# Any two PSUM banks in one relu or clamp, the low-order product planned by itself, first weights multiplied on four quadrants, and a due time for each tile pair

## The chip, the cores and the metric

The kernel runs on one core of a Trainium2 chip. Its time is what the device takes for one execution, in microseconds (us). The number that counts is the median of several runs. An execution under the hardware profiler gives the trace from which the views below are drawn. The core has five engines with an instruction queue each, all of them in order: TensorE (PE, matrix products; its weight loads are shown as PEld), VectorE (DVE), ScalarE (ACT), GpSimd (POOL) and SyncE (SP, which here only issues DMAs). PE writes its results to PSUM, eight banks of 512 floats in each of 128 partitions; DVE and ACT read PSUM, and POOL works on SBUF alone.

## The reference

The input is 4 batches of 12480 tokens with 128 channels, and 32 inducing vectors. Two attention steps are followed by a two-layer network:

```python
def mab(q, kv):
    s = scale * (q @ kv.transpose(0, 2, 1))
    s = s - s.max(-1, keepdims=True)
    a = np.exp(s)
    a /= a.sum(-1, keepdims=True) + 1e-09
    return a @ kv
h = mab(I, x)              # 32 summaries of each batch
y = mab(x, h)              # each token attends to the summaries
z = y.reshape(49920, 128) @ w_in            # 128 -> 2048
g = np.where(z >= 1, z, np.where(z <= -1, 0.0, (z + 1) ** 2 / 4))
out = g @ w_out                             # 2048 -> 128
```

## The kernel before, in words

**Chunks and pairs.** The tokens are cut into 104 chunks of 480 (26 in each batch). The summaries `hT` of a batch are multiplied with `w_in` first, so that the first layer needs only the 32 attention weights of each token: its right side is `hw`, 32 rows for `w_in`'s 2048 columns, kept as an upper and a lower part. The 128 rows of an `hw` tile are two copies of the upper part and two of the lower, and the 128 rows of a chunk's `aT` are upper, lower, upper, lower part of the attention weights, so that one product of 128 rows sums all four. `aT` is filled by four DMAs of 32 rows each, from `a` and `ahi`.

For each chunk there are eight pairs of column tiles, 832 pairs in all. A pair is made in these steps:

1. PE writes two hidden tiles of 128x480 into two PSUM banks (L774).
2. ACT adds 1 and takes the relu of each bank into one half of an SBUF tile `w` (L782).
3. ACT squares all of `w` with a factor of one half (L768).
4. DVE clamps: w = min(max(bank, 1), w) (L787). The two banks are free after that.
5. For six of the eight pairs (`SPLIT`), `w` is rounded to the format fp32r as `hi`, by DVE (L810), ACT (L807) or POOL (L805), and POOL makes `lo` = w - hi (L813).
6. PE adds the pair to the chunk's accumulator (L844): for each half three products, w_lo x hi, w_hi x hi and w_hi x lo; for the two other pairs one product in full float precision, which the trace shows as two records.

There is one accumulator bank. After the last product of a chunk DVE transposes it into `oT` (L854), SP stores it with four DMAs (L858), and only then may the next chunk's first product start. The other seven banks ("h") hold hidden tiles and the scores and summaries of the attention.

**One wide instruction for two banks.** Step 2 and step 4 can be done for both halves in one instruction of 960 elements. Before, that happens only if the two banks are an even one and the next (0 and 1, 2 and 3, 4 and 5), and if both halves are ready when the first is picked; `Slot.pick` looks for such neighbours. Otherwise two instructions of 480 are written.

**The order of the work** is made by a planner when the program is built (`Plan.order`). Each piece of work is added with its engine, an assumed cost, a due time, the work it needs, and the buffer slots it uses. The planner walks through an assumed time; whenever an engine is free it takes, of the work that can start, the one with the smallest due time. Pieces with several engines to choose from (`hi`, and the copy `eN`) go to the engine that gets to them first by this rule. Its result is a fixed list of instructions for each engine; on the chip each engine works through its list and waits for semaphores. Due times before are `STEP` times the pair's number plus an offset from `BEHIND`, one for each kind of work.

**The summaries.** While a batch's chunks run, the next batch is loaded and summarized (`summarize`), and its `hw` tiles are made: four products of 128x512 with `hT` repeated four times over the 128 columns (L634), each cast by ACT (L640), and the lower half of each corrected by DVE (L644). `attend` makes the attention weights of four chunks at a time.

Of the kernel before, what the change touches and what calls it, by code (L numbers as in the profile page):

```python
# [20 lines left out]
    h=7, o=1, xn=9, xT=26, xr=2, e1=1, eN=1, hw=6, w=8, hi=4, lo=4, aT=3, s2=2, a=1, ahi=1, oT=1  # L21
# [8 lines left out]
LEAD = 66950  # L30
STEPS = [0, 1200, 2400, 3600, 8000, 12000, 13000, 18000, 24000, 28000, 32000]

SC = [0, 1200, 2400]
GA = [0, 1500, 6000, 7500]


# [3 lines left out]

KEEP = 0


class Slot:


    def __init__(self, pool, turn=None, near=None):
        self.pool, self.left, self.until, self.place, self.tile = pool, 0, 0, None, None
        self.turn, self.near, self.first = turn, near, False
        if near:  # L50
            near.first = True

    def pick(self, spare, now):

        free = {i for t, i in spare if t <= now}
        if self.near and self.near.place is not None and self.near.place ^ 1 in free:
            return self.near.place ^ 1
        if self.first:
            return min(free, key=lambda i: (i ^ 1 not in free, i % 2, i))
        return min(free, key=lambda i: (i ^ 1 in free, i))  # L60


class Op:


    def __init__(self, engine, cost, lag, due, emit, needs, uses, tiled):
        choice = engine if isinstance(engine, dict) else {engine: (cost, lag, due)}
        self.choice, self.emit, self.uses = choice, emit, uses
        self.engine, self.cost, self.due = None, 0, due
        self.tiled, self.twin, self.merged, self.wide = tiled, None, None, False  # L70
        self.start = self.after = 0
        self.by = {}
        self.unmet, self.then = 0, []
        for n in needs:
            n.then.append(self)
            self.unmet += 1
        for s in self.uses:
            s.left += 1

    def ready(self, engine):  # L80
        return max([self.after, *(t for e, t in self.by.items() if e == engine)])

    def beside(self):

        a, b = self.uses[0].place, self.twin.uses[0].place
        return a % 2 == 0 and b == a + 1


class Plan:
# [5 lines left out]
    def add(self, engine, cost, lag, due, emit, needs=(), uses=(), tiled=False):  # L95
        op = Op(engine, cost, lag, due, emit, [n for n in needs if n], uses, tiled)
        self.ops.append(op)
        return op

    @staticmethod  # L100
    def twins(a, b, cost, lag):

        a.twin, b.twin, a.merged = b, a, (cost, lag)

    def order(self):
        engines = sorted({e for op in self.ops for e in op.choice})
        free = dict.fromkeys(engines, 0)
        able = {e: [] for e in engines}

# [3 lines left out]

        for op in self.ops:
            if not op.unmet:
                enable(op)
        spare = {p: [(0, i) for i in range(n)] for p, n in SLOTS.items()}
        turn = dict.fromkeys(SLOTS, 0)
        tiled = False
        now, done = 0, []  # L120
        while len(done) < len(self.ops):
            later = []
            took = False
            for e in engines:
# [3 lines left out]
                best, rank = None, 0  # L128
                for op in able[e]:
# [12 lines left out]
                    due = op.choice[e][2] - (KEEP if e == "PE" and op.tiled == tiled else 0)  # L142
                    if best is None or due < rank:
                        best, rank = op, due
# [6 lines left out]
                for s in best.uses:  # L151
                    if s.place is None:
                        s.place = s.pick(spare[s.pool], now)
# [3 lines left out]
                if best.merged and best.beside():  # L157
# [6 lines left out]
                if e == "PE" and best.tiled != tiled:  # L164
                    cost, lag, tiled = cost + RETILE, lag + RETILE, best.tiled
                for op in both:
                    op.start, op.engine, op.cost, op.lag = now, e, 0, lag
                    done.append(op)
                best.cost = cost
                free[e] = now + cost  # L170
                later.append(free[e])
                for s in [s for op in both for s in op.uses]:
                    s.left -= 1
                    s.until = max(s.until, now + lag)
                    if not s.left:
                        spare[s.pool].append((s.until, s.place))
                for n in [n for op in both for n in op.then]:
                    n.unmet -= 1
                    if list(n.choice) == [e]:
                        n.after = max(n.after, now + cost + RAW[e])  # L180
                    elif e in n.choice:
                        for x in n.choice:
                            n.by[x] = max(n.by.get(x, 0), now + cost + RAW[e] if x == e else now + lag)
                    else:
                        n.after = max(n.after, now + lag)
                    if not n.unmet:
                        enable(n)
# [7 lines left out]
def attn_moe(  # L195
# [38 lines left out]
        xr=([C, NB, M], F32), e1=([P, CW], F32), eN=([96, 5, P], F32), hw=([P, 512], F32R),  # L234
# [23 lines left out]

    turns = dict.fromkeys(SLOTS, 0)

    def in_turn(pool, near=None):
        turns[pool] += 1
        return Slot(pool, turns[pool] - 1, near)
# [651 lines left out]
```

## Time and profile before

| What | Value |
|---|---|
| median of 3 runs (lowest to highest) | 1773.66 us (1773.36 to 1774.67) |
| the profiled execution | 1771.55 us, of which the trace spans 1769.7 us |
| busy: PE, PEld | 1717.7 us (97%), 1226.7 us (69%) |
| busy: ACT, DVE, POOL | 1695.4 us (96%), 1622.8 us (92%), 1610.4 us (91%) |
| ACT busy in the first 80 us | 9.15 + 12.96 + 4.98 + 11.77 us |
| first relu of a hidden tile on ACT | 72.87 us after the start |
| start of the last square on ACT | 1754.71 us after the start |

PE's matmul records overlap, because one starts before the one ahead of it has left the pipeline, so its busy share is no measure of how full it is; ACT's and DVE's records overlap a little in the same way. How long an engine is held by an instruction is better read as the pitch: the time from its start to the start of the next one, where no wait lies between. The first 75 us load and summarize the first batch. From about 100 us on all engines run the pairs.

### The profile page before, as it was taken

The numbers are of one execution on the slowest core, as the hardware profiler recorded it, in microseconds if no ns is written. First come the engines' busy times: TensorE is split into PE (matmuls) and PEld (weight loads), VectorE is DVE, ScalarE is ACT, GpSimd is POOL, SyncE is SP. The second block draws the span as 40 slices with busy tenths as digits, with TensorE's granted clock in tenths as the row PEclk, the third lists the DMA queues.
The fourth block names the chain that finished last, engine by engine and source line by source line (L and its number), as shares of the span: only waits on it lengthen the run. The fifth ranks groups of instructions, "written<-read, shape, count | busy, mean of one in ns | idle before, by whom it ended". The sixth has DMA issues, their size and how long they took to land.

```text
span 1769.7 us, 26019 instructions
## 1 busy us (share of the span) xinstructions
PE 1717.7 (97%) x7898; PEld 1226.7 (69%) x7898; DVE 1622.8 (92%) x2393; ACT 1695.4 (96%) x2658; POOL 1610.4 (91%) x863
## 2 busy tenths in 40 slices
PE   7699999999999999999999999999999999999998
PEld 5467677777767677776767777677776777777676
DVE  7899889998899898999889999899889999999996
ACT  5599999999999999999999999999999999999997
POOL 0499999999899999999999999999998999999997
PEclk9699999999999999999999999999999999999999
DMA  9532423423232343332233423332211111111111
GB/s 243 98 63 56 79 49 60 72 58 60 44 67 49 62 79 59 65 76 48 47 56 61 72 49 64 70 65 51 45 20 38 34 27 30 35 34 34 33 29 17
DMA packets 425069, 101.78 MB, mean 58 GB/s; under 512 B 369602, under 2 KB 420386, under 8 KB 424930
## 3 DMA queue, kind: packets, MB, share of 16 engines
q1 hardware_dynamic: 424834, 100.01, 30.1%
q8 instruction: 62, 1.02, 0.2%
q14 instruction: 77, 0.63, 0.1%
q10 hardware_dynamic: 96, 0.12, 0.0%
HBM read 48.94 MB, written 25.56 MB: 42 GB/s over the span
## 4 chain that ended last, share of the span: by engine, by line
PE 49%; ACT 25%; DVE 13%; issue 7%; POOL 3%; DMA 2%; SPq 1%; DVEq 0%; POOLq 0%; ACTq 0%
PE banks L844 34%; ACT w L782 13%; PE banks L774 10%; ACT w L768 10%; DVE w L787 7%; DVE hi L810 3%; POOL lo L813 2%; ACT hi L807 1%; PE banks L669 1%; DVE oT L854 1%; PE banks L477 1%; PE banks L530 1%; PE banks L634 1%; SPq L455 1%; POOL hi L805 1%
## 5 line engine op out<-in xcount | busy, mean ns | idle before, releaser
L813 POOL TENSOR_TENSOR lo<-w,hi 128x960 fp32r<-128x960 f32 x624 | 1399.7, 2269 | 63.4 <-DVE hi L810 28.4
L787 DVE SCALAR_TENSOR_TENSOR w<-banks,w 128x480 f32<-128x480 f32 (+1 forms) x1428 | 978.0, 729 | 95.5 <-ACT w L768 85.3
L782 ACT ACTIVATE w<-banks 128x480 f32<-128x480 f32 (+1 forms) x1503 | 889.2, 666 | 12.3 <-PE banks L774 9.5
L768 ACT ACTIVATE w<-w 128x960 f32<-128x960 f32 x832 | 867.0, 1066 | 2.2
L774 PE MATMUL banks<-aT,hw 128*128 128x480 f32 x1664 | 594.9, 431 | 18.2 <-DVE w L787 9.9
L844 PE MATMUL banks<-hi,w_lo 128*128 128x480 f32 x1248 | 538.3, 431 | 9.5 <-DVE oT L854 5.7
L844 PE MATMUL banks<-lo,w_hi 128*128 128x480 f32 x1248 | 474.6, 380 | 1.4 <-POOL lo L813 1.4
L844 PE MATMUL banks<-hi,w_hi 128*128 128x480 f32 x1248 | 474.0, 380 | 0.0
L810 DVE TENSOR_REDUCE hi<-w 128x960 fp32r<-128x960 f32 x373 | 423.7, 1140 | 11.7 <-PE banks L844 0.9
L774 PEld LDWEIGHTS banks<-aT,hw 128*128 128x128 f32 x1664 | 306.7, 189 | 184.1 <-DVE w L787 107.1
L844 PE MATMUL banks<-w,w_f 128*128 128x480 f32 x832 | 393.1, 567 | 0.2 <-DVE oT L854 0.2
L844 PEld LDWEIGHTS banks<-hi,w_lo 128*128 128x128 f32 x1248 | 234.9, 188 | 119.9 <-issue 53.4
L844 PEld LDWEIGHTS banks<-hi,w_hi 128*128 128x128 f32 x1248 | 235.3, 189 | 57.6 <-issue 28.9
L844 PEld LDWEIGHTS banks<-lo,w_hi 128*128 128x128 f32 x1248 | 234.5, 188 | 39.6 <-POOL lo L813 2.9
L844 PEld LDWEIGHTS banks<-w,w_f 128*128 128x128 f32 x832 | 156.1, 189 | 62.6 <-issue 44.3
L805 POOL TENSOR_SCALAR hi<-w 128x960 fp32r<-128x960 f32 x145 | 144.4, 999 | 16.3 <-DVE w L787 9.7
L807 ACT CAST hi<-w 128x960 fp32r<-128x960 f32 x106 | 109.6, 1034 | 7.2 <-PE banks L844 3.3
L854 DVE STREAM_TRANSPOSE oT<-banks 128x480 f32<-128x480 f32 x104 | 70.1, 674 | 7.8 <-PE banks L844 7.5
L403 POOL TENSOR_TENSOR w_lo<-hi,w_hi 128x256 fp32r<-128x256 f32 x6 | 6.5, 1076 | 60.6 <-ACT w_hi L405 60.6
L458 DVE STREAM_TRANSPOSE xT<-xr 128x480 f32<-128x480 f32 x78 | 51.2, 663 | 3.1 <-DMA xr<-in_x 3.0
L712 POOL TENSOR_TENSOR a<-a,ahi 128x480 fp32r<-128x480 f32 (+1 forms) x27 | 33.2, 1231 | 1.3 <-ACT ahi L709 1.3
L530 PE MATMUL banks<-xn,eN 120*32 120x128 f32 (+1 forms) x774 | 31.7, 275 | 0.5 <-ACT eN L522 0.5
(82 smaller groups left out, 553.1 us busy)
## 6 DMA issues: line engine op xcount, KB each, us to landing
out<-oT SPq DMA_DIRECT2D x416, 60.0 KB, 2.2
xn<-in_x SPq DMA_DIRECT2D x93, 240.0 KB, 4.2
xr<-in_x SPq DMA_DIRECT2D x312, 60.0 KB, 2.5
aT<-ahi SPq DMA_DIRECT2D x208, 60.0 KB, 2.0
aT<-a SPq DMA_DIRECT2D x206, 60.0 KB, 2.0
w<-in_x SPq DMA_DIRECT2D x11, 240.0 KB, 4.5
w<-in_moe_w_in SPq DMA_DIRECT2D x8, 256.0 KB, 4.5
w<-in_moe_w_out SPq DMA_DIRECT2D x8, 256.0 KB, 5.3
```

Source lines behind the costliest of these rows:

```text
L458: nc.vector.transpose(make(xT[b, c]), xr.tile.rearrange("c n i -> c (n i)"))
L530: nc.tensor.matmul(p[q * M : (q + 1) * M, :C], eN[g].tile[:, t, q * M : (q + 1) * M], xn[g * Q + q].tile[:, t, :], start=(t == 0), stop=(t ...
L768: nc.scalar.activation(w.tile, w.tile, AF.Square, scale=0.5)
L774: nc.tensor.matmul(make(h)[:, :CW], hw[b][ft // 4].tile[:, ft % 4 * P : (ft % 4 + 1) * P], aT[b, c].tile, start=True, stop=True,)
L782: each(of, i, hs_, w, lambda to, h: nc.scalar.activation(to, h, AF.Relu, bias=1.0))
L787: lambda to, h: nc.vector.scalar_tensor_tensor(to, h, 1.0, to, op0=ALU.max, op1=ALU.min),
L805: nc.gpsimd.tensor_scalar(make(hi), w.tile, 1.0, 0.0, op0=ALU.mult, op1=ALU.add)
L807: nc.scalar.copy(make(hi), w.tile)
L810: nc.vector.tensor_reduce(make(hi), w.tile.unsqueeze(3), axis=AX.X, op=ALU.max)
L813: nc.gpsimd.tensor_sub(make(lo), w.tile, hi.tile.bitcast(F32))
L844: nc.tensor.matmul(acc.tile[:, :CW], wt, g, start=(first and n == 0), stop=(last and n == len(terms) - 1),)
L854: nc.vector.transpose(make(oT).rearrange("c n i -> c (n i)"), acc.tile[:, :CW])
```

## The change

**Any two banks.** `Slot.pick` and `Op.beside` are gone. The two banks of a pair may be any two of the seven; a wide instruction reads them with a step from the lower to the higher bank. Which half of `w`, and which of the two column tiles, a bank holds follows from which of the two banks is the lower (`half`). Where a wide instruction isn't possible yet because the second half isn't ready, the first one's due time is put later by `LONE`.

**The low-order product apart.** The products of a split pair are two pieces of work for the planner instead of one: w_lo x hi and w_hi x hi (`p`), which need only `hi`, and w_hi x lo (`pl`), which needs `lo`.

**First weights on quadrants.** `hT` is kept once (32 columns). One piece of work multiplies it with the four 512-column parts of `w_in`, each into its own 32 partitions of one bank; one ACT cast (`hx`) and one DVE subtraction (`hy`) follow; 16 DMAs on SP's queue copy their 32-row parts into the `hw` tiles.

**Due times.** `BEHIND`, `LEAD`, `STEPS`, `SC` and `GA` become one table `DUE`, with a number for each of the eight pairs of a chunk and each kind of work. `KEEP`, which favours PE work of the same tiling as before, goes from 0 to 450, and assumed costs change by a few ns each.

The diff, cut to its core:

```diff
-BEHIND = {
-    "h": -4400, "r": -3050, "s": -700, "t": 400, "hi": 3700, "hi ACT": 14900, "hi POOL": 9600,
-    "lo": 2200, "p": 9300, "ps": 8900,
+DUE = {
+    "h": [-8100, -3450, -2750, -3300, -3950, 1600, -30300, -35450],
+    "r": [5450, 8600, 10700, -1550, 18200, -11550, -13450, -10800],
...
+LONE = {"r": 300, "t": 150}
-    def beside(self):
-
-        a, b = self.uses[0].place, self.twin.uses[0].place
-        return a % 2 == 0 and b == a + 1
...
+                    if op.merged and not (op.twin in able[e] and op.twin.ready(e) <= now):
+                        due += op.lone
...
-                if best.merged and best.beside():
+                if best.merged:
...
     def each(of, i, hs_, w, do):
         if of[i].wide:
-            do(w.tile, banks[:, hs_[0].place : hs_[0].place + 2, :CW])
+            a, b = sorted(h.place for h in hs_)
+            do(w.tile, banks[:, a : b + 1 : b - a, :CW])
         else:
-            do(w.tile[:, i], hs_[i].tile[:, :CW])
+            do(w.tile[:, half(i, hs_)], hs_[i].tile[:, :CW])
...
-                cost, needs, uses = 3 * 217, [l], [hi, lo]
+                parts = [
+                    ([(w_lo, hi), (w_hi, hi)], 436, "p", [u], [hi]),
+                    ([(w_hi, lo)], 218, "pl", [l], [lo]),
+                ]
             else:
-                hi, lo = w, None
-                cost, needs, uses = 804, ts, [w]
+                parts = [([(w_f, w)], 806, "pf", ts, [w])]
...
+        def multiply():
+            p = make(s_w)
+            for k in range(FF // 512):
+                nc.tensor.matmul(
+                    p[k * M : (k + 1) * M], hT[b], w_in_sb[:, k * 512 : (k + 1) * 512], start=True, stop=True
+                )
+        def upper():
+            nc.scalar.copy(make(wide_hi), s_w.tile)
+        def lower():
+            nc.vector.tensor_sub(make(wide_lo), s_w.tile, wide_hi.tile.bitcast(F32))
...
+            def spread(r, k=k, dst=dst):
+                src = (wide_hi if r < 2 else wide_lo).tile[k * M : (k + 1) * M]
+                nc.sync.dma_start((dst.tile or make(dst))[r * M : (r + 1) * M].bitcast(F32), src.bitcast(F32))
```

How the lists of instructions move is shown at three places. The first is ACT's list some way into the first batch (L782 and L814 are the relu, L768 and L800 the square, L807 the rounding). Before:

```order
L768 ACTIVATE w_1410_5192<-w_1410_5192 128x960
L782 ACTIVATE w_1414_5211<-banks_64 128x480
L768 ACTIVATE w_1414_5211<-w_1414_5211 128x960
L782 ACTIVATE w_1423_5242<-banks_64 128x480 x2
L782 ACTIVATE w_1425_5251<-banks_64 128x480
L768 ACTIVATE w_1423_5242<-w_1423_5242 128x960
L782 ACTIVATE w_1425_5251<-banks_64 128x480
L807 CAST hi_1429_5270<-w_1414_5211 128x960
```

And in the changed kernel:

```order
L814 ACTIVATE w_1401_4938<-banks_64 128x480
L800 ACTIVATE w_1398_4930<-w_1398_4930 128x960
L814 ACTIVATE w_1401_4938<-banks_64 128x480
L814 ACTIVATE w_1406_4955<-banks_64 128x480
L800 ACTIVATE w_1401_4938<-w_1401_4938 128x960
L814 ACTIVATE w_1406_4955<-banks_64 128x480
L814 ACTIVATE w_1414_4978<-banks_64 128x960
L800 ACTIVATE w_1406_4955<-w_1406_4955 128x960
L800 ACTIVATE w_1414_4978<-w_1414_4978 128x960
```

Over the whole program ACT's list goes from 1342 relus of 480 and 161 of 960 to 666 and 499, and from 106 roundings to 69; DVE's from 1192 clamps of 480 and 236 of 960 to 832 of 960, and from 373 roundings to 421; POOL's roundings from 145 to 134.

The second place is PE's list where the 40th chunk ends and the 41st begins (L774 and L806 write hidden tiles, L844 and L871 add to the accumulator; `w_hi7` belongs to a chunk's last pair, `w_lo0` to the first of the next). Before:

```order
L844 MATMUL banks_64<-hi_2017_7317,w_hi7_100 128x480
L844 MATMUL banks_64<-lo_2025_7343,w_hi7_100 128x480
L774 MATMUL banks_64<-aT_1908_6923,hw_1353_4985 128x480 x4
L774 MATMUL banks_64<-aT_1952_7103,hw_1320_4883 128x480
L844 MATMUL banks_64<-hi_2019_7330,w_lo0_89 128x480
L844 MATMUL banks_64<-hi_2019_7330,w_hi0_88 128x480
L844 MATMUL banks_64<-lo_2030_7378,w_hi0_88 128x480
```

And in the changed kernel:

```order
L871 MATMUL banks_64<-hi_2018_6987,w_lo7_101 128x480
L871 MATMUL banks_64<-hi_2018_6987,w_hi7_100 128x480
L871 MATMUL banks_64<-lo_2025_7009,w_hi7_100 128x480 x2
L806 MATMUL banks_64<-aT_1907_6616,hw_1331_4699 128x480 x2
L806 MATMUL banks_64<-aT_1907_6616,hw_1342_4737 128x480 x3
L871 MATMUL banks_64<-hi_2023_7003,w_lo0_89 128x480
L871 MATMUL banks_64<-hi_2023_7003,w_hi0_88 128x480
```

Between the last product of a chunk and the first of the next there stand 4.1 matmuls on average over the 103 handovers before (three in 50 of them), and 5.5 in the changed kernel (five in 58 of them). Behind the last `lo` there now come two products instead of the three of each half.

The third place is SP's list ahead of the first chunk: before, the first chunk's `aT` comes right behind the loads of the next batch.

```order
L455 DMA xr_193_939<-in_x 32x15x32 x4
L733 DMA aT_202_973<-ahi_199_966 32x480 x2
L733 DMA aT_203_980<-ahi_199_966 32x480 x2
L733 DMA aT_203_980<-a_198_963 32x480 x2
L733 DMA aT_207_997<-ahi_199_966 32x480 x2
```

In the changed kernel eleven DMAs for `hw` stand ahead of it:

```order
L669 DMA hw_190_934<-hx_188_927 32x512 x2
L669 DMA hw_190_934<-hy_189_932 32x512 x2
L669 DMA hw_193_945<-hx_188_927 32x512 x2
L669 DMA hw_193_945<-hy_189_932 32x512 x2
L669 DMA hw_195_961<-hx_188_927 32x512 x2
L669 DMA hw_195_961<-hy_189_932 32x512
L760 DMA aT_200_978<-ahi_198_968 32x480 x2
```

What moved there is the queue's order: the first hidden tile needs its `hw` tile and its `aT` from the same queue.

More of the change, by code (lines that the diff above doesn't have):

```diff
@@ L165, in order @@
                     cost, lag, tiled = cost + RETILE, lag + RETILE, best.tiled
+                free[e] = now + cost
+                later.append(free[e])
                 for op in both:
@@ L168, in order @@
                     done.append(op)
+                    left -= 1
+                    finish(op, e, cost, lag)
                 best.cost = cost
[L170 to L187, printed above, removed]
             if not took:
```

256 lines of the change are left out of this document (131 added, 125 removed), and 15 rows, old and new, of the table DUE.

## The prediction

> **What bounds the kernel now.** I read the page's busy shares first, then the busy time by stage, then how the engines stand inside the long middle stage. The page says that no engine is free:
>
> ```profile
> PE 1717.7 (97%) x7898; PEld 1226.7 (69%) x7898; DVE 1622.8 (92%) x2393; ACT 1695.4 (96%) x2658; POOL 1610.4 (91%) x863
> ```
>
> The table by stage (columns: length, then busy time of PE, PEld, DVE, ACT, POOL) puts ACT's idle time at the start:
>
> ```profile
> 60.00:80.00 20.00, 12.34 (x36) 5.46 (x34) 16.37 (x30) 11.77 (x22) 5.82 (x7) 0.67 0.27 54
> ...
> 100.00:1700.00 1600.00, 1580.32 (x7047) 1133.02 (x7046) 1488.42 (x2124) 1579.52 (x2451) 1520.41 (x809) 1.00 0.29 53
> ```
>
> From 100 to 1700 us ACT is idle for only 20 us of 1600, POOL for 80, DVE for 112. PE's 1580 says little, since its records overlap. That ACT isn't merely waiting inside its instructions is seen in its timeline (start, length, instruction), where each starts as soon as the one ahead lets it:
>
> ```profile
> 1743.73 0.99 ACT L782 ACTIVATE w<-banks 128x960 f32<-128x960 f32 x1
> 1744.58 1.02 ACT L807 CAST hi<-w 128x960 fp32r<-128x960 f32 x1
> 1745.46 1.07 ACT L782 ACTIVATE w<-banks 128x480 f32<-128x480 f32 x2
> 1746.37 1.05 ACT L768 ACTIVATE w<-w 128x960 f32<-128x960 f32 x1
> 1747.27 1.07 ACT L782 ACTIVATE w<-banks 128x480 f32<-128x480 f32 x2
> ...
> 1754.00 0.68 ACT L782 ACTIVATE w<-banks 128x480 f32<-128x480 f32 x1
> 1754.71 1.00 ACT L768 ACTIVATE w<-w 128x960 f32<-128x960 f32 x1
> ```
>
> The pitches are 0.85 us for a wide relu, 0.88 for a rounding, 0.45 for a single relu (two in 0.91), 0.90 for a square. The last pair of rows shows a price: the square at 1754.71 works on what the relu at 1754.00 has just written, and starts after 0.71 instead of 0.45 us. With the counts in the view of groups,
>
> ```profile
> L813 POOL TENSOR_TENSOR lo<-w,hi 128x960 fp32r<-128x960 f32 x624 | 1399.7, 2269 | 63.4 <-DVE hi L810 28.4 <-ACT hi L807 8.5 <-PE banks L844 7.4
> L768 ACT ACTIVATE w<-w 128x960 f32<-128x960 f32 x832 | 867.0, 1066 | 2.2
> L782 ACT ACTIVATE w<-banks 128x480 f32<-128x480 f32 x1342 | 733.4, 626 | 11.5 <-PE banks L774 8.7 <-DMA aT<-a 1.2
> L782 ACT ACTIVATE w<-banks 128x960 f32<-128x960 f32 x161 | 160.8, 1002 | 0.8 <-PE banks L774 0.8
> L807 ACT CAST hi<-w 128x960 fp32r<-128x960 f32 x106 | 109.6, 1034 | 7.2 <-PE banks L844 3.3 <-DVE w L787 2.7 <-DVE nm L585 0.6
> L805 POOL TENSOR_SCALAR hi<-w 128x960 fp32r<-128x960 f32 x145 | 144.4, 999 | 16.3 <-DVE w L787 9.7 <-PE banks L844 1.3 <-DVE sm L698 1.1
> ```
>
> ACT's pairs hold it for 1342 x 0.45 + 161 x 0.85 + 832 x 0.90 + 106 x 0.88 = 1583 us. For PE I take the pitch of a matmul, 0.22 us, and of a full-precision product, 0.81 us (803.56 to 804.59 is one of those and one hidden tile):
>
> ```profile
> 800.22 0.38 PE L844 MATMUL banks<-hi,w_lo 128*128 128x480 f32 x1
> 800.44 0.38 PE L844 MATMUL banks<-hi,w_hi 128*128 128x480 f32 x1
> ...
> 803.56 0.97 PE L844 MATMUL banks<-w,w_f 128*128 128x480 f32 x2
> 803.99 0.76 PE L774 MATMUL banks<-aT,hw 128*128 128x480 f32 x1
> 804.59 0.38 PE L844 MATMUL banks<-hi,w_lo 128*128 128x480 f32 x1
> ```
>
> A chunk has 16 hidden tiles, 36 split products and 4 full ones: 52 x 0.217 + 4 x 0.81 = 14.5 us (the quoted starts round 0.217), over 104 chunks 1510. PE also has, in its four largest other groups, 99 us:
>
> ```profile
> L477 PE MATMUL banks<-xT,indT 128*32 128x480 f32 x208 | 29.6, 590 | 0.0
> L669 PE MATMUL banks<-xT,hT 128*32 128x480 f32 x208 | 29.1, 595 | 1.4 <-DVE hw L644 1.0 <-DVE hT L614 0.4
> L530 PE MATMUL banks<-xn,eN 120*32 120x128 f32 x624 | 22.7, 276 | 0.0
> L634 PE MATMUL banks<-w_in_sb,hT 128*128 128x512 f32 x32 | 17.5, 666 | 0.0
> ...
> L494 ACT ACTIVATE e<-banks,nb 128x480 f32<-128x480 f32 x24 | 16.5, 687 | 3.3 <-DVE hi L333 1.7 <-DVE nb L485 0.8 <-PE banks L844 0.8
> L709 ACT CAST ahi<-a 128x480 fp32r<-128x480 f32 x24 | 15.7, 655 | 3.3 <-DVE a L706 3.3
> L689 ACT ACTIVATE s<-s 128x480 f32<-128x480 f32 x24 | 15.1, 630 | 0.1
> L640 ACT CAST hw<-banks 128x512 fp32r<-128x512 f32 x16 | 9.3, 587 | 9.5 <-PE banks L634 9.3
> ```
>
> ACT's four of this kind make 57. So ACT needs some 1640 us, PE some 1609, and POOL 1399.7 + 144.4 = 1544 and its share of the attention. ACT is the bound, and PE stands only 31 us behind it.
>
> **The change part by part.** *Joined relus.* 676 single relus become 338 wide ones: 338 x (2 x 0.45 - 0.85) = 17 us less on ACT. No row shows a wide read of two banks that aren't neighbours. It could cost as much as two singles (gain 0) or as little as the shown one; I take the shown one, since the two banks in the trace already lie a bank's step apart. *Roundings.* 37 fewer on ACT: 37 x 0.88 = 33 us. DVE takes 48 more, POOL 11 fewer (11 x 0.999 = 11 us off). *First weights.* 12 casts fewer on ACT, 12 x 0.58 = 7 us. On PE 16 products (17.5 us) become four groups of four quadrants; L669's 208 records are 28 groups in 29.1 us, 1.04 each, so 4 us remain and 13 go. *Copies `eN`.* Six move from DVE to ACT; with the cast's 0.58 they cost 3.5 us there. *Squares right behind their own relu.* By the lists there are 68 before and 98 after; 30 x 0.26 = 8 us more. ACT in all: -17 - 33 - 7 + 3.5 + 8 = -45 us.
>
> DVE: its pitches stand here.
>
> ```profile
> 803.00 2.34 DVE L787 SCALAR_TENSOR_TENSOR w<-banks,w 128x480 f32<-128x480 f32 x4
> 805.26 1.14 DVE L810 TENSOR_REDUCE hi<-w 128x960 fp32r<-128x960 f32 x1
> 806.31 2.34 DVE L787 SCALAR_TENSOR_TENSOR w<-banks,w 128x480 f32<-128x480 f32 x4
> ...
> 809.63 2.22 DVE L787 SCALAR_TENSOR_TENSOR w<-banks,w 128x960 f32<-128x960 f32 x2
> 811.75 1.15 DVE L810 TENSOR_REDUCE hi<-w 128x960 fp32r<-128x960 f32 x1
> ```
>
> A single clamp is 2.26 / 4 = 0.565, a wide one 2.12 / 2 = 1.06, a rounding 1.05. Joining 596 pairs saves 596 x 0.07 = 42 us; 48 roundings add 51. So DVE, with 112 us idle in the middle stage, stays where it was, and this cover pays for ACT's relief. Roundings right behind their own clamp go from 99 to 141 by the lists; at ACT's 0.26 us for such a neighbour that is 11 us more, under the same cover.
>
> [...]
>
> *The low-order product apart.* It removes no matmul. In the waits,
>
> ```profile
> PEld banks L844 <- DVE oT L854: 25.4, 70, 1.2
> ...
> PE banks L844 <- DVE oT L854: 5.9, 17, 1.1
> ```
>
> PE stands for 31 us at the accumulator's handover. 5.5 instead of 4.1 matmuls stand in a handover now, so 1.4 x 0.217 x 103 = 31 us of other work can fill it. I count it not as a gain by itself but as what lets PE run as full as ACT does now. The price if it doesn't: those 31 us stay, with PE as the bound.
>
> *DMAs for `hw`.* 16 a batch on SP's queue, whose issue takes about 0.62 us each (below: four in 2.46). In the start-up eleven stand ahead of the first `aT`: 6.8 us of issue. The first cast of `hw` ends near 60.9, so they would be out by about 68, when `aT` starts now:
>
> ```profile
> 60.34 0.58 ACT L640 CAST hw<-banks 128x512 fp32r<-128x512 f32 x1 [7.43 <-PE banks L634]
> ...
> 68.46 2.46 SPq L733 DMA_DIRECT2D aT<-ahi  x4
> ```
>
> The chain to `ahi` may be a little earlier, without three of the DVE corrections. I count 0, from -2 to +4. At the three later batches the cover is the ten or so pairs between the last use of an old `hw` tile and the first of the new one, some 20 us for four DMAs; without it each would cost about 5 us.
>
> *The sum.* ACT's need falls by 45 to about 1595. PE's falls by 13 to about 1596. The larger of the two falls from 1640 to 1596, 44 us, but with three engines within a few per cent of each other small waits add up; against that stands the fuller handover. I take 41 off: span 1769.7 - 41 = 1729, profiled 1731, and the median, which is 2 us above the profiled execution, **1732 us**.
>
> **The rivals.** *A. Everything is filled.* If the separate product and the pair-wise due times also take away ACT's 20 us of idle time in the middle stage, 61 go: 1712. For it speaks the handover; against it that PE would then be full to the last us. *B. PE keeps its waits.* If PE is the bound and its 31 us at the handover stay as they are, about 10 of the 41 remain: 1763. For it speaks that PE has never had to run as full; against it the lists, which show more matmuls there. *C. Wide reads at a distance cost two single ones.* Then 17 go on ACT and 42 on DVE: 41 - 17 = 24, so 1750. Nothing in the trace speaks for it. *D. Slower: banks.* A wide clamp frees its first bank 0.5 us later than two singles, and 596 more pairs use one. Seven banks are 3.5 pairs; at 1769.7 / 832 = 2.13 us a pair, a pair may hold its banks for 7.4 us. If that loop decided, half of 0.5 us a bank is 3.4% of 7.4, over 1600 us 54 us, and the time would be 1732 + 54 = 1786. It decides from the point where PE can't write the next tile before ACT asks. For it:
>
> ```profile
> PEld banks L774 <- DVE w L787: 107.1, 295, 1.9
> ...
> ACT w L782 <- PE banks L774: 9.5, 17, 1.5
> ```
>
> The weight load waits for a clamp 295 times; but ACT waits for a hidden tile only 17 times, 9.5 us in all, so the loop has room. *E. Nothing comes of it*, the gain on ACT being eaten by waits: 1773.
>
> **How the numbers follow.** Chances: forecast 0.55 (its own range 1722 to 1745), A 0.15, B 0.10, C 0.06, D 0.09, E 0.05. Faster by over 0.2% (3.5 us, about what a measurement can tell): 0.55 + 0.15 + 0.10 + 0.06 = 0.86. Same 0.05, slower 0.09. The range reaches from below A (1704) over C to 1758, which leaves out D, E and most of B, some 0.2.
>
> **What would show it.** ACT's groups should have the counts above with unchanged pitch: wide relu 0.85, whatever the banks. ACT's busy time should fall by about 45 and the middle stage by about 40 us, with POOL's and PE's weight loads' shares up. If the forecast is right, the waits of PE on the transpose `oT` shrink below 31 us; if B, they stay. D would show as ACT waiting for hidden tiles for over 45 us. The first relu should stand at 71 to 77 us. The forecast is wrong if ACT's idle time between 100 and 1700 us grows by more than the 45 us it gains, or if the wide relu's pitch is near 0.90.

## The result, and the profile after

The changed kernel takes 2354.42 us (median of 4 runs, 2349.28 to 2357.93); the kernel before, run beside it, takes 1773.61 us. The ratio is 1.3271, with a 95% interval of 1.3244 to 1.3297. The forecast was 1732 us, and its range ended at 1758: the kernel became slower by a third instead of faster by 2%.

The page of the changed kernel starts with the busy times of the engines, and gives the shares of the chain of waits by engine and by line:

```profile
PE 1885.5 (80%) x7898; PEld 1259.1 (53%) x7898; DVE 1671.3 (71%) x1827; ACT 1710.5 (73%) x2277; POOL 1600.2 (68%) x852
...
DVE 32%; ACT 29%; PE 27%; issue 6%; POOL 2%; DMA 1%; SPq 1%; DVEq 0%; ACTq 0%; POOLq 0%
```

ACT, POOL and DVE are busy for about as long as before (1710.5 us against 1695.4, 1600.2 against 1610.4, 1671.3 against 1622.8), but in a span that is a third longer: no engine is full any more, and the chain passes in nearly equal shares over three of them. The waits below show them waiting for one another in turn. The table by stage (columns as in the prediction, then PE's granted clock, DMA share and GB/s) says the same of the middle stage:

```profile
100.00:1700.00 1600.00, 1300.80 (x5468) 867.84 (x5469) 1157.41 (x1211) 1204.71 (x1578) 1136.57 (x599) 0.97 0.25 47
1700.00:2300.00 600.00, 474.68 (x1694) 316.38 (x1693) 410.70 (x408) 423.84 (x560) 401.48 (x210) 0.92 0.13 24
```

ACT is idle for 395 us of the 1600, where it was idle for 20; DVE for 443 instead of 112. The view of waits (engine, line, what it waited for: us in total, times, longest) names the pairs. Its five longest rows, shown first, all lie between the three engines that touch the PSUM banks:

```profile
PEld banks L806 <- DVE w L819: 420.7, 382, 3.9
ACT w L814 <- DVE w L819: 351.1, 317, 4.0
DVE w L819 <- ACT w L814: 341.9, 311, 2.6
PE banks L806 <- DVE w L819: 252.4, 248, 3.1
PEld banks L806 <- ACT w L814: 224.7, 168, 4.3
...
ACT w L814 <- PE banks L806: 173.5, 220, 2.4
...
PE banks L806 <- ACT w L814: 144.8, 136, 3.9
...
DVE w L819 <- PE banks L806: 105.8, 98, 3.3
```

The second row is the one to look at. A relu (L814) needs a hidden tile from PE and a free buffer `w`, which another engine has read last; from the clamp of another pair it needs nothing. In the trace of before no row of this view has a relu waiting for a clamp. Here it happens 317 times. The third row looks like one of before, where a clamp waits for the square of its own pair (L768):

```profile
DVE w L787 <- ACT w L768: 85.3, 124, 2.9
```

but L814 is no square: the clamp now waits for a relu. The view of groups shows that the wide instructions wait, and the narrow ones too:

```profile
L819 DVE SCALAR_TENSOR_TENSOR w<-banks,w 128x960 f32<-128x960 f32 x832 | 954.0, 1154 | 574.2 <-ACT w L814 341.9 <-PE banks L806 105.8 <-ACT w L800 96.8
...
L814 ACT ACTIVATE w<-banks 128x960 f32<-128x960 f32 x499 | 480.9, 971 | 330.0 <-DVE w L819 230.3 <-PE banks L806 79.1 <-POOL lo L845 5.2
...
L814 ACT ACTIVATE w<-banks 128x480 f32<-128x480 f32 x666 | 366.0, 570 | 219.1 <-DVE w L819 120.8 <-PE banks L806 94.4 <-POOL lo L845 1.5
```

**One stretch, instruction by instruction.** The timelines of ACT, of DVE and of PE (in this order) between 807 and 816 us:

```profile
807.11 0.97 ACT L814 ACTIVATE w<-banks 128x960 f32<-128x960 f32 x1 [1.01 <-DVE mx L708]
807.98 1.89 ACT L800 ACTIVATE w<-w 128x960 f32<-128x960 f32 x2
810.28 0.97 ACT L814 ACTIVATE w<-banks 128x960 f32<-128x960 f32 x1 [0.41 <-DVE w L819]
811.15 0.59 ACT L716 ACTIVATE s<-s 128x480 f32<-128x480 f32 x1
...
812.54 0.96 ACT L814 ACTIVATE w<-banks 128x960 f32<-128x960 f32 x1
```

```profile
809.01 2.22 DVE L819 SCALAR_TENSOR_TENSOR w<-banks,w 128x960 f32<-128x960 f32 x2 [0.24 <-ACT w L800]
...
813.60 1.16 DVE L819 SCALAR_TENSOR_TENSOR w<-banks,w 128x960 f32<-128x960 f32 x1 [1.17 <-POOL lo L845]
```

```profile
814.81 1.14 PE L806 MATMUL banks<-aT,hw 128*128 128x480 f32 x4 [1.94 <-DVE w L819]
```

The trace has no bank numbers, but the built program has, and its instructions stand in the same order. With them, and with the instruction that raises the counter to the value that each waits for:

```
start   end     instruction              banks   waits last for         its banks
806.36  807.00  DVE maximum (attention)  5
807.11  808.08  ACT relu                 4, 6    that maximum           5
809.01  810.17  DVE clamp                0, 2
810.28  811.26  ACT relu, another pair   1, 3    that clamp             0, 2
812.54  813.50  ACT relu                 0, 5
813.60  814.76  DVE clamp of the pair    1, 3    that relu              0, 5
814.81          PE hidden tile           2       that clamp             1, 3
```

(DVE's row at 809.01 merges two clamps; the first is the one in the table.) The relu of banks 1 and 3 starts 0.12 us after the end of a clamp of banks 0 and 2, with which it shares no bank and no tile. Before the second clamp of 1 and 3 DVE stands idle for 1.17 us until a relu of 0 and 5 is over; the square of its own pair had ended at 812.64, so some 0.9 us of this are owed to the relu. (The profile's row names POOL there; the program waits for a `lo` too, but that one ended at 805.75.) PE then stands idle for 1.94 us and writes bank 2 when the clamp of 1 and 3 is over. In each case the bank, or one of the banks, lies between the other instruction's two.

**All waits.** I did the same for each wait of the program. Of each instruction that waits, I compared its banks and tiles with those of the instruction that it waits for. Waits for which there is no common bank and no common tile, but a bank of the one between the lower and the higher bank of the other: before none, in the changed kernel 1767 (DVE for ACT 460, ACT for DVE 430, DVE for PE 295, PE for DVE 249, PE for ACT 234, ACT for PE 74, DVE for itself 25). Two instructions that only read are ordered in this way too. So, as far as the waits tell, the framework that writes the semaphores treats a read of banks a and b with a step as if it touched all banks from a to b. 403 of the 499 wide relus and 672 of the 832 wide clamps are of two banks that aren't neighbours.

Joined with the trace, this tells which wait ended each idle stretch of over 0.05 us between 100 and 1700 us: us idle in all, and in brackets how much of it was ended by a wait of that kind.

| Engine | before | changed kernel | changed, distant pairs split (e1) |
|---|---|---|---|
| ACT | 18 (0) | 393 (279) | 19 (0) |
| DVE | 109 (0) | 440 (335) | 53 (0) |
| PE | 19 (0) | 299 (252) | 14 (0) |

The rest of the idle time ends with waits that have a reason, for a hidden tile or for the pair's own square, which can be late because of the others; the runs don't part that.

### The profile page after: what moved, and what is told of

Same layout as the page of the kernel before. It is cut to its first block, busy times and chain, and to the rows that moved or that the text cites. A ratio compares the mean times of both kernels' runs of the same rounds, so it can differ in the third digit from the quotient of the medians.

```text
span 2355.8 us, 25210 instructions
## 1 busy us (share of the span) xinstructions
PE 1885.5 (80%) x7898; PEld 1259.1 (53%) x7898; DVE 1671.3 (71%) x1827; ACT 1710.5 (73%) x2277; POOL 1600.2 (68%) x852
## 4 chain that ended last, share of the span: by engine, by line
DVE 32%; ACT 29%; PE 27%; issue 6%; POOL 2%; DMA 1%; SPq 1%; DVEq 0%; ACTq 0%; POOLq 0%
DVE w L819 27%; ACT w L814 20%; PE banks L871 14%; PE banks L806 10%; ACT w L800 8%; DVE hi L842 3%; POOL lo L845 1%; PE banks L491 1%; PE banks L696 1%; PE banks L544 1%; ACT hi L839 0%; DVE banks L702 0%; DMA w<-in_moe_w_in 0%; SPq L669 0%; DVE oT L883 0%
## 5 line engine op out<-in xcount | busy, mean ns | idle before, releaser
L819 DVE SCALAR_TENSOR_TENSOR w<-banks,w 128x960 f32<-128x960 f32 x832 | 954.0, 1154 | 574.2 <-ACT w L814 341.9
L814 ACT ACTIVATE w<-banks 128x480 f32<-128x480 f32 (+1 forms) x1165 | 835.4, 741 | 549.1 <-DVE w L819 351.1
L806 PE MATMUL banks<-aT,hw 128*128 128x480 f32 x1664 | 665.8, 455 | 414.9 <-DVE w L819 252.4
L800 ACT ACTIVATE w<-w 128x960 f32<-128x960 f32 x832 | 814.3, 1003 | 3.1
L806 PEld LDWEIGHTS banks<-aT,hw 128*128 128x128 f32 x1664 | 310.0, 196 | 741.5 <-DVE w L819 420.7
L871 PE MATMUL banks<-hi,w_lo 128*128 128x480 f32 x1248 | 509.5, 408 | 6.0 <-DVE oT L883 5.2
L871 PE MATMUL banks<-hi,w_hi 128*128 128x480 f32 x1248 | 494.0, 396 | 0.0
L842 DVE TENSOR_REDUCE hi<-w 128x960 fp32r<-128x960 f32 x421 | 478.4, 1141 | 17.3 <-PE banks L871 5.0
L871 PE MATMUL banks<-lo,w_hi 128*128 128x480 f32 x1248 | 422.5, 413 | 0.5 <-POOL lo L845 0.5
L871 PE MATMUL banks<-w,w_f 128*128 128x480 f32 x832 | 402.0, 583 | 0.0
L871 PEld LDWEIGHTS banks<-lo,w_hi 128*128 128x128 f32 x1248 | 247.0, 200 | 73.5 <-issue 35.4
L871 PEld LDWEIGHTS banks<-hi,w_lo 128*128 128x128 f32 x1248 | 247.7, 198 | 71.6 <-issue 22.9
L871 PEld LDWEIGHTS banks<-hi,w_hi 128*128 128x128 f32 x1248 | 247.4, 198 | 44.9 <-issue 6.5
L871 PEld LDWEIGHTS banks<-w,w_f 128*128 128x128 f32 x832 | 162.3, 195 | 63.4 <-issue 45.7
L839 ACT CAST hi<-w 128x960 fp32r<-128x960 f32 x69 | 68.3, 990 | 13.2 <-DVE w L819 12.1
L728 POOL TENSOR_TENSOR s<-s,sm 128x480 f32<-128x480 f32 (+1 forms) x27 | 27.0, 998 | 25.4 <-DVE sm L725 20.3
L491 PE MATMUL banks<-xT,indT 128*32 128x480 f32 x208 | 29.9, 608 | 15.4 <-DVE w L819 13.3
```

Of the source, the lines that this page charges most:

```text
L491: nc.tensor.matmul(p[q * M : (q + 1) * M, :CW], indT, xT[b, c].tile, start=True, stop=True)
L800: nc.scalar.activation(w.tile, w.tile, AF.Square, scale=0.5)
L806: nc.tensor.matmul(make(h)[:, :CW], hw[b][ft // 4].tile[:, ft % 4 * P : (ft % 4 + 1) * P], aT[b, c].tile, start=True, stop=True,)
L814: each(of, i, hs_, w, lambda to, h: nc.scalar.activation(to, h, AF.Relu, bias=1.0))
L819: lambda to, h: nc.vector.scalar_tensor_tensor(to, h, 1.0, to, op0=ALU.max, op1=ALU.min),
L839: nc.scalar.copy(make(hi), w.tile)
```

## The experiments

Three theories went into them. Theory 1: the waits for banks in between cost the time. Theory 2: joining itself does, because a wide instruction holds two banks longer (rival D of the prediction). Theory 3: one of the other parts does, the low-order product, the first weights or the due times.

**e1: distant pairs split.** The changed kernel's plan and order, with a wide instruction over banks that aren't neighbours written as two of 480:

```diff
             a, b = sorted(h.place for h in hs_)
-            do(w.tile, banks[:, a : b + 1 : b - a, :CW])
+            if b - a == 1:
+                do(w.tile, banks[:, a : b + 1, :CW])
+            else:
+                do(w.tile[:, 0], banks[:, a, :CW])
+                do(w.tile[:, 1], banks[:, b, :CW])
```

> The changed kernel with its plan and order of work kept; only where a wide relu or clamp would read two banks that aren't neighbours, two instructions of 480 are written in its place. Theory 1 (a wide instruction over banks a and b is given the waits of every bank from a to b, so engines wait for work on banks in between that they never touch): these waits go, the 403 distant relus cost 0.05 us more each on ACT (20 us), the 672 distant clamps 0.07 us more on DVE (47 us, under idle time), so 1740 to 1790 us, and ACT's waits for a clamp fall from 351 us to below 30. Theory 2 (joining itself: a joined pair holds both of its seven banks too long): the plan still waits for both banks, so at most a part comes back, 2000 us or more. Theory 3 (the separate low-order product, the DMAs for the first weights or the table of due times are to blame, not the joining): stays near 2300 us.

Measured: 1747.95 us, ratio to before 0.9866 (0.985 to 0.9883). All of the loss is gone, with the changed kernel's order otherwise kept, and the kernel is 1.3% faster than before. Its page and its middle stage:

```profile
PE 1699.4 (97%) x7898; PEld 1227.9 (70%) x7898; DVE 1656.3 (95%) x2499; ACT 1666.9 (95%) x2680; POOL 1600.2 (92%) x852
...
100.00:1700.00 1600.00, 1586.09 (x7135) 1147.78 (x7135) 1544.61 (x2258) 1577.40 (x2516) 1530.76 (x806) 1.00 0.30 55
```

and of its waits those that answer to the rows above (its relu is L818, its clamp L823):

```profile
PEld banks L810 <- DVE w L823: 76.0, 252, 2.6
...
DVE w L823 <- ACT w L804: 32.6, 59, 1.5
...
ACT w L818 <- PE banks L810: 10.9, 19, 1.7
```

No row of this view has a relu waiting for a clamp. This refutes theory 3 and agrees with theory 1, but with theory 2 as well, since it takes joins away.

**e2: as many joins, on neighbours.** The two banks of a pair are always taken together and are neighbours, so that all 832 clamps and 702 pairs of relus are joined, more than in the changed kernel, and no wait for a bank in between is left:

```diff
+        if self.mate is None:
+            return min(free, key=lambda i: (-lone(i), i))
+        i = min((i for i in free if i + 1 in free), key=lambda i: (-lone(i) - lone(i + 1), i))
+        self.mate.place = i + 1
+        return i
...
+            hs_[0].mate = hs_[1]
```

> The changed kernel, planned with the rule that the two banks of a pair are always taken together and are neighbours (any parity): all 832 clamps are wide and 702 of the relus, and none spans a bank in between. Theory 1: no false waits, so far below 2354, about 1760 to 1860 us (the due times weren't made for this rule, and two free banks that aren't neighbours can't be used). Theory 2: more joining than in the changed kernel on fewer usable banks, so as slow as it or slower, 2300 us or more. Theory 3: about 2300 us as well.

Measured: 1814.24 us, in a single run. That is 42 us more than before and 540 less than the changed kernel, with more joins. Theory 2 can't make up the loss. For the 42 us the groups and waits of this kernel point to another cause:

```profile
L828 ACT ACTIVATE w<-banks 128x960 f32<-128x960 f32 x702 | 667.1, 982 | 1.2 <-PE banks L820 0.8 <-POOL hi L851 0.2
...
L853 ACT CAST hi<-w 128x960 fp32r<-128x960 f32 x179 | 179.7, 1004 | 16.0 <-DVE w L833 13.9 <-PE banks L885 1.9
```

```profile
DVE w L833 <- ACT w L814: 173.3, 239, 3.0
...
ACT w L828 <- PE banks L820: 11.9, 29, 0.8
```

This order gives ACT 179 roundings, where before it had 106. By the prediction's pitches ACT's pairs need 260 x 0.45 + 702 x 0.85 + 832 x 0.90 + 179 x 0.88 = 1620 us, 37 more than the 1583 of before: 541 more joins saved 27 us and 73 more roundings added 64. DVE then waits for ACT's squares (L814 here). My expectation, 1760 to 1860 us, had left the roundings out.

**e3: any two banks alone.** Theory 1 says that the first part of the change is harmful by itself. This is the kernel before with that part alone, without the new due times:

```diff
-                if best.merged and best.beside():
+                if best.merged:
...
-            do(w.tile, banks[:, hs_[0].place : hs_[0].place + 2, :CW])
+            a, b = sorted(h.place for h in hs_)
+            do(w.tile, banks[:, a : b + 1 : b - a, :CW])
```

> The kernel before with one part of the change alone: any two banks may be joined (478 clamps and 158 relus then reach over a bank in between, 354 and 162 are neighbours). Theory 1: slower by a good part of what the change lost, 1950 to 2250 us, with ACT and PE waiting for clamps of other pairs. Theory 2: slower too, about 1800 to 1900, with PE alone waiting for its own banks. Theory 3: no slower than before, 1750 to 1780 us.

Measured: 2092.34 us in a single run, 320 more than before. The kernel has 478 clamps and 158 relus over distant banks, and 1014 waits for a bank in between. The same kinds of waits stand up (relu L787, clamp L792):

```profile
PE banks L779 <- DVE w L792: 188.7, 226, 2.3
DVE w L792 <- ACT w L787: 188.3, 191, 4.0
ACT w L787 <- DVE w L792: 144.7, 161, 2.7
```

**e4 and e7: the other parts alone.** The kernel before with the low-order product planned apart (e4), and with the first weights on quadrants and their DMAs (e7). The core of each edit:

```diff
-                cost, needs, uses = 3 * 217, [l], [hi, lo]
+                parts = [
+                    ([(w_lo, hi), (w_hi, hi)], 436, BEHIND["ps"], [u], [hi]),
+                    ([(w_hi, lo)], 218, BEHIND["ps"], [l], [lo]),
+                ]
```

> The kernel before with one other part alone: the product with the lower part is a piece of work by itself, with the due times of before. Theories 1 and 2: this part is harmless, 1755 to 1785 us, and the handover of the accumulator is a little fuller. Theory 3: if this part is to blame, clearly slower, 1900 us or more.

```diff
-            hT[b] = const.tile([C, Q, M], F32, name=f"hT_{b}")
+            hT[b] = const.tile([C, M], F32, name=f"hT_{b}")
...
+        m = add("PE", 910, 1100, end + 1, multiply, [hT_made[b], *in_made], [s_w, wide_hi, wide_lo], tiled=True)
+        u = add("ACT", 480, 620, end + 1, upper, [m], [wide_hi, s_w])
+        l = add("DVE", 640, 780, end + 2, lower, [u], [s_w, wide_hi, wide_lo])
```

> The kernel before with the first weights' part alone: one product on four quadrants, one cast, one subtraction and 16 DMAs for each batch, due times of before. ACT loses 12 casts (7 us), PE 13 us, SP gains 64 DMAs; the plan may place other work where that was. If the parts add up as costed, 1763 to 1772 us; if the DMAs in front of the first chunk's right side cost what the changed kernel's later first relu shows (74.05 against 72.87 us), 1 us of it is lost; slower than 1780 would say that this part does harm.

Measured: e4 1773.6 us, ratio 1.0007 (0.9998 to 1.0017); e7 1774.74 us, ratio 1.001 (1.0 to 1.0019). Neither does anything that can be told from no change. For e7 that misses what was expected, 1763 to 1772 us: its 12 casts fewer don't show in the time. Its plan puts six more copies `eN`, two more roundings and 11 fewer joined relus on ACT, which takes up part of them; the rest stays open.

**e5 and e6: a dose.** The changed kernel's order again. In e5 only the distant clamps stay wide (672) and the distant relus are split; in e6 only the distant relus stay wide (403). The edit is that of e1, with a condition in front, which of the two kinds is split:

```diff
-            do(w.tile, banks[:, a : b + 1 : b - a, :CW])
+            if b - a == 1 or of is not hs_.far:
+                do(w.tile, banks[:, a : b + 1 : b - a, :CW])
+            else:
+                do(w.tile[:, 0], banks[:, a, :CW])
+                do(w.tile[:, 1], banks[:, b, :CW])
```

> The changed kernel with its plan and order kept; distant relus are written as two of 480, distant clamps stay wide (672 of them). In the built program 1327 waits are left whose only ground is a bank in between, against 1767 in the changed kernel and none in the run with both split. If each false wait costs about alike, as between those two runs ((2354 - 1748) / 1767 = 0.34 us), 1748 + 1327 x 0.34 = 2200 us; 2050 to 2300. If only the relus' false waits mattered, near 1750.

> The other half: distant clamps are written as two of 480, distant relus stay wide (403). 870 false waits are left, so 1748 + 870 x 0.34 = 2046 us by the same price; 1880 to 2150. If only the clamps' false waits mattered, near 1750.

Measured: e5 2135.75 us, e6 1983.37 us, one run each. Against e1 they cost 388 and 235 us; together 623, where the changed kernel has 606 over e1. The waits follow the kind that was left wide. In e5 PE waits for clamps, in e6 for relus, and in both ACT waits for clamps (L815 writes hidden tiles, L828 is the clamp, L823 the relu):

```profile
PE banks L815 <- DVE w L828: 260.6, 285, 2.9
ACT w L823 <- DVE w L828: 226.8, 231, 2.7
```

```profile
PE banks L815 <- ACT w L823: 129.2, 152, 2.9
ACT w L823 <- DVE w L828: 128.0, 157, 2.4
```

Set against the number of waits for a bank in between:

| Kernel | such waits | us over the kernel without them | us a wait |
|---|---|---|---|
| e6 | 870 | 235 (over e1) | 0.27 |
| e3 | 1014 | 320 (over before) | 0.32 |
| e5 | 1327 | 388 (over e1) | 0.29 |
| changed | 1767 | 606 (over e1) | 0.34 |

**e8, e9 and e10: what the change is worth without those waits.** e8 joins two banks only where they are neighbours of either parity, lets the choice of banks look for neighbours, and has due times made anew for this rule; e9 is e1 once more, beside it; e10 is e8 with the changed kernel's due times.

```diff
-                if best.merged:
+                if best.merged and best.beside():
...
+    def pick(self, spare, now):
+        free = {i for t, i in spare if t <= now}
+        side = lambda i: [j for j in (i - 1, i + 1) if j in free]
+        if self.near and self.near.place is not None:
+            by = [i for i in free if abs(i - self.near.place) == 1]
+            if by:
+                return min(by, key=lambda i: (len(side(i)), i))
...
-    "r": [5450, 8600, 10700, -1550, 18200, -11550, -13450, -10800],
+    "r": [-4250, 2200, 12100, -5200, 19200, -11950, -13400, -13200],
```

> The changed kernel, but relus and clamps are joined only when their two banks are neighbours (of either parity), the choice of banks prefers such neighbours, and the due times are made anew for that rule: 337 wide relus and 513 wide clamps, where the kernel of e1_split_far has 96 and 160. No instruction waits for work whose only common ground is a bank in between. Theory 1 (only the banks in between cost, and ACT's need sets the end otherwise): ACT's pairs need 990 x 0.45 + 337 x 0.85 + 832 x 0.90 + 71 x 0.88 = 1543 us, 10 less than e1_split_far's 1553 and 40 less than before, so about 1738 to 1744 us, with ACT idle for some 20 us between 100 and 1700. Theory 2 (joining itself holds banks too long): with three times as many joins it is slower than e1_split_far, over 1755. Rival B of the prediction (PE bounds at the handover): no better than e1_split_far, 1745 to 1750, and ACT idle for over 30 us in the middle stage.

> The kernel of e1_split_far again, on the same chip and beside the same runs as e8_next_due, so that the two can be set against each other to within less than one per cent: 1747 to 1750 us by every theory.

> The kernel of e8_next_due with the changed kernel's own due times: 348 wide relus and 517 wide clamps, all on neighbours, as many as in e8_next_due, but 93 roundings on ACT instead of 71. It tells whether e8_next_due's gain came from the joins or from the order that the due times make. If ACT's need sets the end once no wait is owed to a bank in between: 968 x 0.45 + 348 x 0.85 + 832 x 0.90 + 93 x 0.88 = 1562 us, 21 less than before, so 1748 to 1757 us, some 17 more than e8_next_due, all of it from the roundings. If the joins were what counts: as fast as e8_next_due, 1733 to 1740. If due times that were made for another rule of joining cost waits of their own: over 1760, with ACT idle for over 35 us between 100 and 1700.

Measured: e8 1734.97 us, ratio 0.9781 (0.9768 to 0.9794); e9 1750.75 us, ratio 0.9867 (0.9854 to 0.9881); e10 1755.14 us, ratio 0.9893 (0.9877 to 0.991). e8 is the fastest of all, 38 us under before and 3 us under the band that was expected of it; e9 is 0.75 us over its own. e8's middle stage, its relus and its waits (L830 is the relu, L822 writes hidden tiles, L887 adds to the accumulator, L899 is the transpose):

```profile
100.00:1700.00 1600.00, 1587.98 (x7179) 1155.10 (x7178) 1528.16 (x1927) 1574.80 (x2296) 1549.78 (x823) 1.00 0.30 56
```

```profile
L830 ACT ACTIVATE w<-banks 128x480 f32<-128x480 f32 x990 | 536.8, 603 | 16.8 <-PE banks L822 15.1 <-POOL lo L861 0.2
...
L830 ACT ACTIVATE w<-banks 128x960 f32<-128x960 f32 x337 | 329.7, 993 | 0.9 <-PE banks L822 0.5 <-POOL lo L861 0.2
```

```profile
PEld banks L887 <- DVE oT L899: 22.6, 55, 1.0
...
ACT w L830 <- PE banks L822: 15.6, 27, 1.4
...
PE banks L887 <- DVE oT L899: 6.4, 16, 1.0
```

ACT is idle for 25 us of the 1600, about as little as before (20): it is the bound again, and the time has followed what it has to do. e10 has as many joins as e8 and 20 us more; the row of its roundings has 93 of them, where e8 has 71:

```profile
L855 ACT CAST hi<-w 128x960 fp32r<-128x960 f32 x93 | 94.2, 1013 | 7.6 <-DVE w L835 5.5 <-PE banks L822 1.1 <-DVE banks L717 0.7
```

That fits the pitches: 22 more roundings make 19 us. So what e8's own due times bring is above all where the roundings go, and by the pitches one rounding (0.88 us) is worth as much as some eighteen joins (0.05 each).

**ACT's need against the time.** With the prediction's pitches (0.45, 0.85, 0.90 and 0.88 us) and each kernel's own counts of single relus, wide relus and roundings (832 squares in all of them):

| Kernel | counts | ACT's need | time | time - need |
|---|---|---|---|---|
| before | 1342, 161, 106 | 1583 | 1772.0 to 1773.6 | 189 to 191 |
| e4 | 1310, 177, 107 | 1583 | 1773.6 | 191 |
| e7 | 1364, 150, 108 | 1585 | 1774.7 | 190 |
| e10 | 968, 348, 93 | 1562 | 1755.1 | 193 |
| e1, e9 | 1472, 96, 69 | 1553 | 1748.0, 1750.8 | 195, 197 |
| e8 | 990, 337, 71 | 1543 | 1735.0 | 192 |
| e2 | 260, 702, 179 | 1620 | 1814.2 | 194 |
| e3 | 1024, 320, 116 | 1584 | 2092.3 | 509 |
| changed | 666, 499, 69 | 1533 | 2354.4 | 821 |

Where no wait is owed to a bank in between, the time is ACT's need plus 189 to 197 us, over 77 us of difference in need. e8 and e10 had been forecast by this sum before they ran. Where such waits exist, the rule is gone.

## Why the prediction was wrong, step by step

- **The step that failed** is the one on the joined relus (and, with it, on the joined clamps): "No row shows a wide read of two banks that aren't neighbours. It could cost as much as two singles (gain 0) or as little as the shown one". Both ends were durations of the instruction. The cost sat in the waits that such an instruction gets and gives, and these were bounded by nothing: 1767 waits, 606 us over e1. Such a wide read is no costlier in itself: the relus of banks 4 and 6 and of banks 1 and 3 at 807.11 and 810.28 above hold ACT for 0.87 us each, as far as the next start. The median of this pitch is 0.868 us for the relus of distant banks and 0.856 for those of neighbours in the same trace. So rival C falls too, and my term of 17 us was of the right size. What stood to be looked at was the list of waits of the built program: before, a relu far into the program waits for PE or a buffer of `w`; in the changed one many wait for DVE as well (462 of 1165 relus, against 42 of 1503 before). I read that list for the order of the instructions and not for what they wait for.
- **Rival D**, the slower one, had the place right (banks) and the mechanism wrong. It priced how long a wide clamp holds its own two banks. Its sign, ACT waiting for hidden tiles for over 45 us, did show (173.5 us), but e2 has more joins, only 11.9 us of that wait and no such loss: a sign that two mechanisms share tells neither. The sentence "ACT waits for a hidden tile only 17 times, 9.5 us in all, so the loop has room" was true of the list as it was, and no evidence on waits that the edit adds.
- **ACT as the bound, and its sum.** Right where the waits in between are taken away. The forecast took 41 us off; e8 has 38 less with a need that is 40 lower, e1 has 24 less with 30. In the changed kernel itself the need fell by 50 (1583 to 1533), and nothing of it arrived. By the last table it would take an estimated 1533 + 189 to 197 = 1722 to 1730 us without the waits; no run shows this, and that e8, a kernel with another plan, lands near the forecast of 1732 is no confirmation of it. One reading in the sum was off: ACT's fourth largest other group is not the casts of `hw` (9.3 us) but the copies `xT` of the first batch (L443, 14.0 us), so that ACT's four make 61 us and not 57. The forecast doesn't hang on it.
- **Roundings**, 33 of the 45 us: the count is that of the built lists, and it was the largest term of all. e10 against e8 bears out the price: 22 more of them, with 11 more joins, cost 20 us, where the pitches make 19.
- **The saving of a join.** By the trace's pitches it is 0.05 us (two single relus in 0.90, a wide one in 0.85). By them e2, with 541 more wide relus than before, saves 27 us there, and its time fits that: time - need is 194, like the others.
- **The handover.** I said that more matmuls between two chunks would let PE run as full as ACT, and that its waits on `oT` would shrink below 31 us. In the changed kernel they do (14.7 and 5.2 us), but only because PE waits elsewhere. In e1, with the same order, they are 31.5 us on the weight loads and 6.2 on the products, more than before:

```profile
PEld banks L875 <- DVE oT L887: 31.5, 69, 1.0
...
PE banks L875 <- DVE oT L887: 6.2, 17, 0.7
```

  and in e8 they are 22.6 and 6.4, hardly less than before. (What the next chunk's first product waits for is DVE's transpose; it needn't wait for the store of `oT`, as the description of the kernel has it.) The time was ACT's all the same, so this step wasn't needed; it is not shown that the product planned apart helps at all (e4: nothing). Rival B (PE keeps its waits and bounds at 1763) is refuted by e1 and e8, which are faster than that.
- **The first weights' DMAs.** I counted 0, from -2 to +4 us, and the first relu at 71 to 77 us. It starts at 74.05, 1.2 us later than before, behind the `aT` that left SP's queue at 69.62. But single traces can't price this part: e1, e9, e5 and e6 have the same lists up to there, and their first relu starts at 73.94, 75.65, 71.89 and 78.25 us; in e7, with this part alone, it starts at 72.84, as before. The rows of the changed kernel:

```profile
69.62 1.17 SPq L760 DMA_DIRECT2D aT<-ahi  x2
```

```profile
74.05 1.03 ACT L814 ACTIVATE w<-banks 128x480 f32<-128x480 f32 x2 [0.43 <-PE banks L806]
```

- **What would make it wrong** was named: ACT's idle time between 100 and 1700 us growing by more than the 45 us it gains. It grew by 375.

## What to carry to other kernels

An edit that changes which memory an instruction touches can change whom it waits for and who waits for it (here from no wait for a bank in between to 1767): before its duration is counted, list the waits of that instruction in the built program and ask of each what the two have in common. An access with a step over a shared tile may be ordered as if it touched all that lies between, as the 403 relus and 672 clamps of distant banks were here, so give the two halves neighbouring places, or write two instructions: a join here saved 0.05 us and a wait cost 0.3 on average. When the bound is an engine with a plain sum of pitches, check the sum on several variants; here, with about 190 us added for all else, it gave every undisturbed time to within 8 us.

## What the runs showed that I had not expected

The ordering by range holds between two reads too: in 890 of the 1767 waits (460 and 430) an instruction of DVE and one of ACT wait for each other although both only read PSUM; in 827 of them it is a relu and a clamp. Whether the chip itself would need any of these waits isn't shown. No run here kept the distant wide reads and left out the waits: each kernel that has the one has the other, 870 waits (e6) to 1767.

PE's granted clock, 1.00 in the middle stage of e1 and e8, is 0.97 in that of the changed kernel and 0.92 between 1700 and 2300 us, in the rows by stage above. That comes along with PE's idle time (299 us between 100 and 1700, against 14 in e1); how much of the 606 us it adds is open, as is why a wait costs 0.34 us with 1767 of them and 0.27 with 870.
